# Local attention in an attention-and-FFN kernel: sums of values moved directly behind the next unit's scores

## The chip, the cores and the metric

The kernel runs on one core of a Trainium2 chip. The metric is the device time of one execution in microseconds. TensorE (PE; its weight loads are rows of PEld), VectorE (DVE), ScalarE (ACT), GpSimd (POOL) and SyncE (SP, which issues the transfers) each work through a queue of their own and wait for each other by semaphores.

## The reference, cut to what matters

For 8 batches and 8 heads of 64 columns, 512 local queries see 32 global keys and the local keys at most 32 positions away; 32 global queries see everything. The 8 heads side by side (512 columns) then go through a norm and a feed-forward network of 2048 hidden columns with a residual.

```python
s_g = scale * np.matmul(q_g, k_all.transpose(0, 1, 3, 2))
out_g = np.matmul(sm(s_g), v_all)
mask = np.abs(pos[:, None] - pos[None, :]) <= window      # window = 32
s_ll = np.where(mask, scale * np.matmul(q_l, k_l.transpose(0, 1, 3, 2)), -1e9)
s_lg = scale * np.matmul(q_l, k_g.transpose(0, 1, 3, 2))
out_l = np.matmul(sm(np.concatenate([s_lg, s_ll], axis=-1)), np.concatenate([v_g, v_l], axis=2))
...
xn = (x - mu) / np.sqrt(var + 1e-06) * g_ln
out = x + np.maximum(xn @ w_ch1, 0.0) @ w_ch2
```

## The kernel before

**Units.** Local attention is cut into 64 units (class `Local`): a batch, a pair of heads, one half of 256 local rows. A unit has three stages.

- `scores` (L248): 16 matmuls in the program (32 instructions in the trace) of 64 rows by 32 columns of the array into the left 256 columns of two PSUM banks, `sc[0]` for the pair's first head and `sc[1]` for its second. Then, on VectorE and ScalarE, four reductions with the mask (`p<-sc`, L275) and four exponentials (L285).
- `transposes` (L289): units 8 to 15 on TensorE (`tp`) with a copy by ScalarE, units 16 to 63 as 16 transposes on VectorE (`pt<-p`, L307).
- `values` (L309): 16 matmuls (32 instructions) of 128 rows by 32 columns into a third bank, `pv`; then VectorE writes `x<-pv` (L328, one instruction). At its end `values` loads the operands of the unit after the next (`u<-in_eu`, L245) into the one of two buffers that it has read. After a pair's fourth unit, `finish` stores x (`xs<-x`) and makes the norm: statistics (L189, L191), `rs` by GpSimd and VectorE, and `x<-x` on ScalarE (L202).

The scores' banks, `tp`, `pv` and the chunks' transposes `t` all turn in one PSUM pool of two banks (`ps_a`, tag `att`).

**Chunks.** Rows go through the feed-forward network in nine chunks: 0 to 7 of four tiles of 128 local rows (eight units each), 8 of the global rows. `ffn` loops over 16 slabs f of the hidden columns: `mm1(f)` is 12 matmuls of 512 columns into `ph`, followed by `hh` (ScalarE, L539) and `hl` (VectorE, L540); then come 12 matmuls of `mm2(f-1)` into `acc`. `mm2(f)`, which has `hl(f)` as its weights, thus stands behind `mm2(f-1)` and `mm1(f+1)`. At a chunk's end its output goes out (`out<-ob`, four transfers) and the next chunk's residual comes into the same buffers (`ob<-xs`, four transfers).

**Order.** Units 0 to 7 run ahead of the network. The other units stand in it: while chunk c runs, the units of chunk c+1 are computed, and in chunks 1 to 5 also the first unit of chunk c+2. `PLACES` says where: place 2f is `mm1(f)`, 2f+1 is `mm2(f-1)`; unit n of a chunk starts at int(start + n * period), and its three stages stand 0, 1 and 4 places further (0, 2 and 3 in chunk 0; start 1, period 3.75 in chunks 2 to 6). At place 1 there is no `mm2`, since f is 0 there. The stages are generators of which `ffn` takes a step ahead of each third of `mm1` and each quarter of `mm2`. The order on TensorE and SyncE is the program's; VectorE, ScalarE and GpSimd are ordered by the scheduler.

Of the kernel before, what the change touches and what calls it, by code (L numbers as in the profile page):

```python
# [31 lines left out]

ON_PE = 16

PLACES = {0: (0, 3.5, (0, 2, 3)), 1: (0, 3.4, (0, 1, 4)), 7: (1, 3.5, (0, 1, 2)), 9: (1, 3.75, (0, 1, 4))}
BIG = 3.0e38


# [8 lines left out]
def attention_ffn_kernel(  # L47
# [12 lines left out]
    B, HP, _, _, _ = eu.shape  # L60
# [159 lines left out]
    class Local:  # L220


        def __init__(self, b, hp, half, alone, on_pe):
            self.at = b, hp, half
            self.alone = alone
            self.on_pe = on_pe
            self.next = None

        def bank(self, k, name):

# [18 lines left out]
        def scores(self):  # L249
            half = self.at[2]  # L250
            mn = small.tile([P, 4], F32, name="mn")
            self.sm = small.tile([P, 4], F32, name="sm")
            self.p = self.ap.tile([P, 4, P], F32, name="p", bufs=3)
            sc = [self.bank(h, "sc") for h in range(2)]
            for qb in range(2):
                for g in range(4):
                    gp = slice(g * WIN, (g + 1) * WIN)
                    w = 4 * qb + g
                    k0 = 8 + w + w // 3
                    for h in range(2):  # L260
                        hd = slice(h * D, (h + 1) * D)
                        nc.tensor.matmul(  # L262
                            sc[h][gp, qb * P:(qb + 1) * P],
                            self.e[hd, w * WIN:(w + 1) * WIN],
                            self.e[hd, k0 * WIN:(k0 + 4) * WIN],
                            start=True,
                            stop=True,
                            tile_position=(h * D, g * WIN),
                            skip_group_check=True,
                        )  # L270
            yield
            for h in range(2):
                for qb in range(2):
                    c = 2 * h + qb
                    nc.vector.tensor_tensor_reduce(  # L275
                        out=self.p[:, c],
                        in0=sc[h][:, qb * P:(qb + 1) * P],
                        in1=masks[half, qb],
                        scale=-QSCALE,
                        scalar=BIG,  # L280
                        op0=ALU.add,
                        op1=ALU.min,
                        accum_out=mn[:, c:c + 1],
                    )
                    nc.scalar.activation(  # L285
                        self.p[:, c],
                        self.p[:, c],
                        AF.Exp,
                        bias=mn[:, c:c + 1],  # L289
                        scale=-1.0,  # L290
                        accum_out=self.sm[:, c:c + 1],
                    )
# [15 lines left out]

        def values(self):  # L309
            b, hp, half = self.at  # L310
            pv = self.bank(3, "pv")
            for h in range(2):
                for qb in range(2):
                    for g in range(4):
                        gp = slice(g * WIN, (g + 1) * WIN)
                        nc.tensor.matmul(  # L316
                            pv[gp, qb * P + h * D:qb * P + h * D + D],
                            self.pt[:, 2 * h + qb, gp],
                            self.v[:, 4 * qb + g, h * D:(h + 1) * D],
                            start=True,  # L320
                            stop=True,
                            tile_position=(0, g * WIN),
                            skip_group_check=True,
                        )
            ri = small.tile([P, 4], F32, name="ri")
            nc.gpsimd.tensor_scalar(ri, self.sm, SUM_EPS, None, ALU.add)  # L326
            nc.vector.reciprocal(ri, ri)
            nc.vector.tensor_tensor(  # L328
                self.x[:, :, hp * P:(hp + 1) * P].rearrange("p q (h d) -> p q h d", h=2),
                pv[:, :256].rearrange("p (q h d) -> p q h d", q=2, h=2),  # L330
                ri.rearrange("p (h q) -> p q h", h=2).unsqueeze(3).to_broadcast([P, 2, 2, D]),
                op=ALU.mult,
            )
            if not self.alone and self.next and self.next.next:
                self.next.next.load()
# [141 lines left out]
    def rows_local(b, t):  # L477
        r0 = b * SA + SG + t * P
        return [(slice(0, P), r0, P)]

    def rows_global(bg):
        return [(slice(i * SG, (i + 1) * SG), (bg * BG + i) * SA, SG) for i in range(BG)]

    def transpose_chunk(xn, out, t0=0, nt=None):


        n = len(xn) * P
        nt = nt or len(xn)
        for kt in range(KT):
            t = ps_a.tile([P, 512], F32, name="t", tag="att")  # L490
            for j in range(len(xn)):
                nc.tensor.transpose(  # L492
                    t[:, j * P:(j + 1) * P], xn[j][:, kt * P:(kt + 1) * P], ident
                )
            if t0 == 0:
                u = kt % 2
                if u == 0:
                    his = fpool.tile([P, 2, 512], F32R, name=f"xh{kt}", tag=f"xh{kt}")
                    if nt > 2:
                        los = fpool.tile([P, 2, 512], F32R, name=f"xl{kt}", tag=f"xl{kt}")  # L500
                out.append((his[:, u], los[:, u]) if nt > 2 else (his[:, u, :256], his[:, u, 256:]))
            hi, lo = (a[:, t0 * P:t0 * P + n] for a in out[kt])
            gk = g_sb[:, kt:kt + 1]
            nc.scalar.activation(hi, t[:, :n], AF.Copy, scale=gk)
            nc.vector.scalar_tensor_tensor(
                lo, t[:, :n], gk, f32(hi), ALU.mult, ALU.subtract
            )
            yield
# [87 lines left out]
    def tiles(c):  # L596
        return tiles_of(ready.pop(c))
# [5 lines left out]
    last_chunk = len(chunks) - 1  # L603
# [12 lines left out]
    units = sum(phases, [])  # L616
    need = [sum(u.chunk <= c for u in units) for c in range(len(chunks))]
# [40 lines left out]

    def stages(units):

        for u in units:
            def first(u=u):
                yield from u.scores()

            def second(u=u):
                for _ in u.transposes():
                    pass
                return
                yield

            def third(u=u):
                for _ in values(u):
                    pass
                yield

            yield first, second, third

    queue = list(stages(units[need[0]:]))
    queue.reverse()

# [4 lines left out]
    with tc.manual_schedule(engines={ET.SP}):  # L685
# [6 lines left out]
        with hurry(True):  # L692
            scores = [u.scores() for u in units[:need[0]]]
# [33 lines left out]
    for c, chunk in enumerate(chunks):  # L727
        if c == 0:
            ctx.enter_context(tc.manual_schedule(engines={ET.PE}))
        if chunk is None:  # L730
            rows = [rows_global(bg) for bg in range(NBG)]
        else:
            rows = [rows_local(b, 2 * half + j) for b, half in chunk for j in range(2)]
        want = need[min(c + 1, last_chunk)] + (0 < c < last_chunk - 2)
        count = want - traced["units"]
        traced["units"] = want
        start, period, offs = PLACES.get(c, PLACES[9])
        at = {}
        place = 0
        for n in range(count):  # L740
            for o, run in zip(offs, queue.pop()):
                place = min(max(int(start + n * period) + o, place), 2 * NF - 1)
                at.setdefault(place, []).append(run)

        def stage(f, k, at=at, c=c):
            if c == 0 and k == 0:
                for _ in weights_to(f + SPLIT_AHEAD + 1, LOADS_AHEAD):
                    pass
            for run in at.get(2 * f + k, ()):
                yield from run()  # L750

        nxt = []

        def next_chunk(c=c, nxt=nxt):
            if c + 1 < len(chunks):
                yield from transpose_chunk(tiles(c + 1), nxt)

        ffn(c, xt, rows, stage, next_chunk)
        xt = nxt
# [87 lines left out]
```

## Time and profile before

| | us |
|---|---|
| median of 3 runs | 998.15 |
| lowest and highest | 997.3 and 999.79 |
| the profiled execution | 995.42 |
| its span, first to last instruction | 993.6 |
| TensorE busy in the span | 948.8 |
| VectorE, ScalarE, GpSimd busy | 578.0, 314.7, 44.0 |

Matmuls overlap their own ends, so busy time says little of the pace. What a stretch costs is read from the starts of the instructions behind it.

### The profile page before, as it was taken

To read this page: it belongs to the slowest core of one execution; us is meant where nothing else is said; L and a number is where in the kernel's file an instruction comes from. 1 tells how busy PE (TensorE), PEld (TensorE's weight loads), DVE (VectorE), ACT (ScalarE), POOL (GpSimd) and SP (SyncE) were. 2 spreads that over 40 slices of the span, in tenths; PEclk is the share of its full clock that TensorE was granted. 3 is DMA by queue.
4 is the path that set the end of the run, shared out by engine and by line. 5 is a ranking of instruction groups with operands and counts; after the bars stand their busy time and mean duration, and the time that the engine had idled before them with its cause. 6 is when DMAs were issued, how large, how long until landed. Compare 5 with 4: busy or idle time off the path is not lost.

```text
span 993.6 us, 21066 instructions
## 1 busy us (share of the span) xinstructions
PE 948.8 (95%) x8616; PEld 717.2 (72%) x8616; DVE 578.0 (58%) x1873; ACT 314.7 (32%) x842; POOL 44.0 (4%) x150
## 2 busy tenths in 40 slices
PE   6569999999999999999999999999999989999997
PEld 4347677677777777777777777777777766766796
DVE  4589943666766666766666666766666642222311
ACT  5677743223222223222322222222222231232210
POOL 3000000000000000000000000000000000000000
PEclk9679999999999999999999999999999999999999
DMA  8565632323232224222332224222322344543110
GB/s 357 203 250 203 231 113 85 121 76 119 97 120 75 89 80 149 90 93 71 104 122 84 101 68 146 93 71 93 123 84 86 108 158 150 191 147 136 44 32 22
DMA packets 31872, 118.80 MB, mean 120 GB/s; under 512 B 4256, under 2 KB 6304, under 8 KB 27680
## 3 DMA queue, kind: packets, MB, share of 16 engines
q1 hardware_dynamic: 31776, 117.46, 34.6%
q8 instruction: 68, 1.11, 0.5%
q14 instruction: 28, 0.23, 0.1%
HBM read 99.62 MB, written 17.83 MB: 118 GB/s over the span
## 4 chain that ended last, share of the span: by engine, by line
PE 85%; DMA 3%; DVE 3%; ACT 2%; issue 1%; SPq 0%; POOL 0%; ACTq 0%; DVEq 0%
PE acc L550 37%; PE ph L531 36%; PE sc L262 4%; PE pv L316 3%; DMA raw<-in_wd 2%; PE t L492 1%; PE pv L419 1%; DMA xs<-x 1%; PE sc L371 1%; PE t L407 1%; DVE tmp L142 0%; DVE hl L540 0%; DVE pt L307 0%; DVE tmp L146 0%; ACT p L285 0%
## 5 line engine op out<-in xcount | busy, mean ns | idle before, releaser
L550 PE MATMUL acc<-w,hh 128*128 128x512 f32 x1088 | 342.7, 396 | 0.0
L531 PE MATMUL ph<-xh,w 128*128 128x512 f32 (+1 forms) x1216 | 311.7, 382 | 0.0
L307 DVE STREAM_TRANSPOSE pt<-p 32x128 f32<-32x128 f32 x768 | 232.5, 303 | 62.2 <-ACT p L285 50.1
L531 PEld LDWEIGHTS ph<-xh,w 128*128 128x128 f32 x1216 | 214.0, 188 | 49.8 <-issue 3.1
L550 PEld LDWEIGHTS acc<-w,hh 128*128 128x128 f32 x1088 | 205.7, 189 | 44.4
L550 PE MATMUL acc<-w,hl 128*128 128x512 f32 x544 | 225.7, 415 | 2.9 <-DVE hl L540 2.9
L539 ACT ACTIVATE hh<-ph 128x512 fp32r<-128x512 f32 (+1 forms) x144 | 82.3, 572 | 355.6 <-PE ph L531 354.4
L540 DVE SCALAR_TENSOR_TENSOR hl<-ph,hh 128x512 fp32r<-128x512 f32 (+1 forms) x144 | 94.3, 656 | 164.9 <-ACT hh L539 163.4
L285 ACT ACTIVATE p<-p,mn 128x128 f32<-128x128 f32 x256 | 99.7, 391 | 187.9 <-DVE mn L275 187.9
L531 PE MATMUL ph<-xl,w 128*128 128x512 f32 x512 | 143.4, 401 | 0.0
L550 PEld LDWEIGHTS acc<-w,hl 128*128 128x128 f32 x544 | 102.4, 188 | 32.7 <-issue 7.2
L531 PEld LDWEIGHTS ph<-xl,w 128*128 128x128 f32 x512 | 94.0, 188 | 27.8 <-issue 6.9
L275 DVE CUSTOM_DVE_ANT_0 p<-sc,mask 128x128 f32<-128x128 f32 x256 | 58.9, 285 | 45.4 <-PE sc L262 44.8
L262 PE MATMUL sc<-u 64*32 64x128 f32 x2048 | 58.1, 293 | 13.0 <-DMA u<-in_eu 6.2
L262 PEld LDWEIGHTS sc<-u 64*32 64x32 f32 x2048 | 32.3, 112 | 41.6 <-issue 25.1
L316 PEld LDWEIGHTS pv<-u,pt 128*32 128x32 f32 x2048 | 33.8, 113 | 28.1 <-issue 22.4
L328 DVE TENSOR_TENSOR x<-pv,ri 128x256 f32<-128x256 f32 x64 | 26.8, 420 | 43.6 <-PE pv L316 43.6
L316 PE MATMUL pv<-u,pt 128*32 128x64 f32 x2048 | 45.7, 228 | 3.1 <-ACT pt L301 3.0
L285 ACT ACTIVATION_READ_ACCUMULATOR p<-p,mn 128x1 f32 x256 | 47.9, 187 | 0.0
L326 POOL TENSOR_SCALAR ri<-sm 128x4 f32<-128x4 f32 x64 | 17.4, 272 | 585.1 <-ACT p L285 580.9
L202 ACT ACTIVATE x<-x,rs 128x512 f32<-128x512 f32 x32 | 24.8, 811 | 45.1 <-DMA xs<-x 43.5
L492 PE MATMUL t<-ident,x 128*128 128x128 f32 x136 | 23.1, 290 | 10.1 <-DVE x L207 3.9
(58 smaller groups left out, 442.0 us busy)
## 6 DMA issues: line engine op xcount, KB each, us to landing
u<-in_eu SPq DMA_DIRECT2D x63, 848.0 KB, 4.7
raw<-in_wd SPq DMA_DIRECT2D x16, 1024.0 KB, 5.4
gk<-in_gk SPq DMA_DIRECT2D x8, 1088.0 KB, 5.0
xs<-x SPq DMA_DIRECT2D x32, 256.0 KB, 5.7
ob<-xs SPq DMA_DIRECT2D x32, 256.0 KB, 3.4
out<-ob SPq DMA_DIRECT2D x32, 256.0 KB, 2.1
gv<-in_gv SPq DMA_DIRECT2D x8, 1024.0 KB, 5.0
u<-in_eu SPq DMA_DIRECT2D x1, 512.0 KB, 4.1
```

The source lines that it names most:

```text
L202: nc.scalar.activation(x[:, j, :], x[:, j, :], AF.Identity, bias=rs[:, 1, j:j + 1], scale=rs[:, 0, j:j + 1],)
L262: nc.tensor.matmul(sc[h][gp, qb * P:(qb + 1) * P], self.e[hd, w * WIN:(w + 1) * WIN], self.e[hd, k0 * WIN:(k0 + 4) * WIN], start=True, sto ...
L275: nc.vector.tensor_tensor_reduce(out=self.p[:, c], in0=sc[h][:, qb * P:(qb + 1) * P], in1=masks[half, qb], scale=-QSCALE, scalar=BIG, op0= ...
L285: nc.scalar.activation(self.p[:, c], self.p[:, c], AF.Exp, bias=mn[:, c:c + 1], scale=-1.0, accum_out=self.sm[:, c:c + 1],)
L307: nc.vector.transpose(out=self.pt[rp, :, gp], in_=self.p[gp, :, rp])
L316: nc.tensor.matmul(pv[gp, qb * P + h * D:qb * P + h * D + D], self.pt[:, 2 * h + qb, gp], self.v[:, 4 * qb + g, h * D:(h + 1) * D], start= ...
L328: nc.vector.tensor_tensor(self.x[:, :, hp * P:(hp + 1) * P].rearrange("p q (h d) -> p q h d", h=2), pv[:, :256].rearrange("p (q h d) -> p ...
L492: nc.tensor.transpose(t[:, j * P:(j + 1) * P], xn[j][:, kt * P:(kt + 1) * P], ident)
L531: nc.tensor.matmul(ph[:, :n], w[:, kt, :], xx[kt][:, :n], start=(i == 0), stop=(i == 3 * KT - 1),)
L539: nc.scalar.activation(hh[:, :n], ph[:, :n], AF.Relu)
L540: nc.vector.scalar_tensor_tensor(hl[:, :n], ph[:, :n], 0.0, f32(hh[:, :n]), ALU.max, ALU.subtract)
L550: nc.tensor.matmul(acc[t], a[:, ts], w, start=(f == 0 and i == 0), stop=(f == NF - 1 and i == 2),)
```

## The change

The sums of values of unit n-1 no longer have a stage of their own. They stand directly behind the score matmuls of unit n, and they go into the right half (columns 256 to 511) of that unit's bank `sc[0]` in place of a bank `pv`. The first unit of the queue (unit 8) has no unit ahead; the last local unit (63) and the global units keep their third stage. So 55 units' sums move. Chunk 0 takes nine units in place of eight, and chunk 1 eight in place of nine, with the places of the other chunks. The instructions are as many as before on every engine.

```diff
-PLACES = {0: (0, 3.5, (0, 2, 3)), 1: (0, 3.4, (0, 1, 4)), 7: (1, 3.5, (0, 1, 2)), 9: (1, 3.75, (0, 1, 4))}
+PLACES = {0: (0, 3.5, (0, 2, 3)), 7: (1, 3.5, (0, 1, 2)), 9: (1, 3.75, (0, 1, 4))}
...
-            sc = [self.bank(h, "sc") for h in range(2)]
+            sc = self.sc = [self.bank(h, "sc") for h in range(2)]
...
         def values(self):
             b, hp, half = self.at
-            pv = self.bank(3, "pv")
+
+            pv = self.beside.sc[0][:, 256:] if self.beside else self.bank(3, "pv")
...
-        for u in units:
-            def first(u=u):
-                yield from u.scores()
+
+        for n, u in enumerate(units):
+            before = units[n - 1] if n else None
+            if before and u.chunk == last_chunk and before.chunk < last_chunk:
+                before = None
+            alone = n + 1 == len(units) or u.chunk == last_chunk or units[n + 1].chunk == last_chunk
+
+            def first(u=u, before=before):
+                scores = u.scores()
+                if before and u.chunk < last_chunk:
+                    next(scores)
+                    before.beside = u
+                    for _ in values(before):
+                        pass
+                yield from scores
...
-            yield first, second, third
+            yield (first, second, third) if alone else (first, second)
...
-        want = need[min(c + 1, last_chunk)] + (0 < c < last_chunk - 2)
+        want = need[min(c + 1, last_chunk)] + (c < last_chunk - 2)
```

TensorE, chunk 3, before its second unit's scores. Before, sums and scores stand apart, with three network matmuls between them:

```order
L531 MATMUL ph<-xl_4114,w 128x512 x2
L531 MATMUL ph<-xh_4091,w 128x512 x2
L531 MATMUL ph<-xh_4113,w 128x512 x2
L316 MATMUL pv<-u,pt 32x64 x16
L550 MATMUL acc_4147<-w,hl 128x512
L550 MATMUL acc_4147<-w,hh 128x512 x2
L262 MATMUL sc<-u 32x128 x16
L550 MATMUL acc_4148<-w,hl 128x512
```

The same unit now (line numbers are one higher from L309 on):

```order
L551 MATMUL acc_4101<-w,hl 128x512
L551 MATMUL acc_4101<-w,hh 128x512 x2
L551 MATMUL acc_4102<-w,hl 128x512
L551 MATMUL acc_4102<-w,hh 128x512 x2
L262 MATMUL sc<-u 32x128 x16
L317 MATMUL sc<-u,pt 32x64 x16
L532 MATMUL ph<-xh_4040,w 128x512 x2
L532 MATMUL ph<-xh_4062,w 128x512 x2
```

Scores and sums are one block. At a chunk's head the second unit's scores now stand 24 network matmuls behind the first unit's (one `mm1`, one `mm2`), where before 39 matmuls and a block of sums lay between them; elsewhere 36 or 48 stand between two units.

SyncE's queue at the same chunk's head, before:

```order
L245 DMA u<-in_eu 128x1696
L583 DMA out<-ob 128x512 x4
L559 DMA ob<-xs 128x512 x4
L245 DMA u<-in_eu 128x1696 x3
L342 DMA xs<-x 128x512 x2
```

And now:

```order
L343 DMA xs<-x 128x512 x2
L584 DMA out<-ob 128x512 x4
L560 DMA ob<-xs 128x512 x4
L245 DMA u<-in_eu 128x1696 x4
L343 DMA xs<-x 128x512 x2
```

The load for the chunk's second unit, which stood ahead of the four stores and four loads, stands behind them.

VectorE, third unit of chunk 3, from its last reductions to `hl`, before:

```order
L275 ISA p,mn<-sc,mask_105 128x128
L275 ISA mn 128x1
L307 STREAM_TRANSPOSE pt<-p 32x4x32 x9
L540 SCALAR_TENSOR_TENSOR hl<-ph,hh 128x512
L307 STREAM_TRANSPOSE pt<-p 32x4x32 x7
L327 RECIPROCAL ri<-ri 128x4
L540 SCALAR_TENSOR_TENSOR hl<-ph,hh 128x512
L328 TENSOR_TENSOR x<-pv,ri 128x2x128
```

And now:

```order
L275 ISA p,mn<-sc,mask_105 128x128
L275 ISA mn 128x1
L329 TENSOR_TENSOR x<-sc,ri 128x2x128
L275 ISA p,mn<-sc,mask_96 128x128
L275 ISA mn 128x1
L275 ISA p,mn<-sc,mask_105 128x128
L275 ISA mn 128x1
L307 STREAM_TRANSPOSE pt<-p 32x4x32 x16
L328 RECIPROCAL ri<-ri 128x4
L541 SCALAR_TENSOR_TENSOR hl<-ph,hh 128x512 x2
```

The write of x now stands between the reductions of `sc[1]` and those of `sc[0]`, and both `hl` stand behind all 16 transposes. In a chunk's fourth unit, and in its last one, the norm's statistics stand ahead of the transposes as well.

## Rows read from the trace of the kernel before

**Rows 1.** The page: busy time of TensorE, and its granted clock by slices.

```profile
PE 948.8 (95%) x8616; PEld 717.2 (72%) x8616; DVE 578.0 (58%) x1873; ACT 314.7 (32%) x842; POOL 44.0 (4%) x150
PEclk9679999999999999999999999999999999999999
```

**Rows 2.** Lines L262 and L316: duration of one, ns min/median/max.

```profile
L262 PE MATMUL sc<-u x2048: 266/269/420, 3.8 to 779.5; 64*32 64x128 f32 x187
...
L316 PE MATMUL pv<-u,pt x2048: 219/219/316, 14.3 to 790.9; 128*32 128x64 f32 x187
```

**Rows 3.** TensorE in order of time, chunk 4: start us, us, instruction.

```profile
506.28 1.09 PE L531 MATMUL ph<-xl,w 128*128 128x512 f32 x4
507.22 1.10 PE L531 MATMUL ph<-xh,w 128*128 128x512 f32 x4
508.24 0.65 PE L316 MATMUL pv<-u,pt 128*32 128x64 f32 x32
...
509.16 0.63 PE L550 MATMUL acc<-w,hh 128*128 128x512 f32 x2
509.72 1.06 PE L262 MATMUL sc<-u 64*32 64x128 f32 x32
510.71 0.50 PE L550 MATMUL acc<-w,hl 128*128 128x512 f32 x1
511.05 0.63 PE L550 MATMUL acc<-w,hh 128*128 128x512 f32 x2
...
518.05 0.63 PE L550 MATMUL acc<-w,hh 128*128 128x512 f32 x2
...
520.32 0.67 PE L262 MATMUL sc<-u 64*32 64x128 f32 x32
...
521.96 1.09 PE L531 MATMUL ph<-xh,w 128*128 128x512 f32 x4
```

**Rows 4.** Waits from 173 to 800 us: total us, times, longest.

```profile
PEld sc L262 <- DVE x L328: 4.7, 18, 0.3
```

**Rows 5.** TensorE ahead of the network: scores and sums without network matmuls between.

```profile
25.84 1.17 PE L262 MATMUL sc<-u 64*32 64x128 f32 x32
26.95 0.31 PE L316 MATMUL pv<-u,pt 128*32 128x64 f32 x6
```

**Rows 6.** Head of chunk 3 in order of time: TensorE, SyncE's queue, VectorE.

```profile
393.88 0.67 PE L262 MATMUL sc<-u 64*32 64x128 f32 x32
...
400.18 1.10 PE L531 MATMUL ph<-xh,w 128*128 128x512 f32 x4
...
394.60 1.75 SPq L559 DMA_DIRECT2D ob<-xs  x4
...
397.23 5.10 DVE L307 STREAM_TRANSPOSE pt<-p 32x128 f32<-32x128 f32 x16 [1.09 <-ACT p L285]
```

**Rows 7.** Landing of the load of u issued at 403.8, nothing ahead of it.

```profile
DMA to landing us min/median/max: 4.9/4.9/4.9
```

**Rows 8.** Four loads of ob, and the load of u behind them: issue, landing.

```profile
L559 SPq DMA_DIRECT2D ob<-xs x4: 326/428/430, 131.3 to 132.6; - x4
...
L245 SPq DMA_DIRECT2D u<-in_eu x1: 333/333/333, 134.0 to 134.0; - x1
...
DMA to landing us min/median/max: 6.4/6.4/6.4
```

**Rows 9.** Chunk 0: TensorE in order; waits 58 to 170; window: PE busy, PEclk, DMA.

```profile
120.68 0.62 PE L550 MATMUL acc<-w,hh 128*128 128x512 f32 x2
...
126.45 0.39 PE L550 MATMUL acc<-w,hl 128*128 128x512 f32 x1
...
PEld sc L262 <- DVE x L328: 2.4, 3, 1.5
...
123.00:125.00 2.00, 2.00 (x33) 0.50 0.79 221
```

**Rows 10.** VectorE, statistics of a norm in chunk 4.

```profile
532.58 1.29 DVE L189 BATCH_NORM_STATS2 st<-x 128x6 f32<-128x512 f32 x2
```

More of the change, by code (lines that the diff above doesn't have):

```diff
@@ L226, in __init__ @@
             self.on_pe = on_pe
-            self.next = None
+            self.next = self.beside = None
         def bank(self, k, name):
```

## The prediction

> **What bounds the kernel now.** I read the page first: TensorE is busy for 95% of the span, and its granted clock is full (2.4 GHz) in nearly every slice [rows 1]. So what counts is the order of starts on TensorE. Next I read that order in a steady chunk [rows 3]. Four network matmuls take 0.94 us from start to start (506.28 to 507.22), so one takes 0.234. A block of small matmuls breaks this pace twice, going in and coming out, and where an unbroken pace would have put a later matmul tells what the block costs. Last I looked at what TensorE waits for [rows 4], and at the head of a chunk [rows 6], where the change puts two units closest together. The sum is made against the profiled execution, 995.42 us, of which 993.6 is span; that is 2.7 below the median of the runs, 998.15, and I carry the difference over.
>
> **One block in place of two.** The second `hh` matmul behind the sums should start at 507.22 + 0.94 + 0.23 = 508.39 without them; it starts at 509.16 [rows 3]. So the sums cost 0.77 us. From 518.05, where two `hh` matmuls, sums, four matmuls, scores and four matmuls follow, ten matmuls alone would lead to 520.39, and the trace has 521.96: both blocks cost 1.57, and so scores 0.80. Taken apart: scores start 0.09 us later than a network matmul would (509.72 against 509.16 + 0.47 = 509.63). The burst takes 0.67 - 0.27 = 0.40 from first to last start [rows 2, 3]. From a burst's last start to the next network matmul is 0.20 (509.72 + 1.06 - 0.27 = 510.51 to 510.71), and the second network matmul follows 0.34 behind the first (511.05), 0.10 too late. The sums show the same entry: 508.24 against 507.22 + 0.94 = 508.16.
>
> With sums directly behind scores three things go: 0.20 (leaving the scores), 0.10 (the late second matmul) and 0.09 (entering the sums). What comes is the step from scores to sums. Ahead of the network it is there: the last of 32 scores starts at 25.84 + 1.17 - 0.27 = 26.74, the sums at 26.95, so 0.20 [rows 5]. The saving is 0.39 - 0.20 = 0.19 us a unit, and for 55 units **10.5 us**. The ends: nothing if the step costs as much as what goes, 21 if it costs nothing; the row shows the very step, so I take it.
>
> **Waits for a bank that go.** Scores wait in the middle of their burst where `x<-pv` has not yet left a bank of the shared pool: 18 times from 173 to 800 us [rows 4]. At 509.72 the burst lasts 1.06 in place of 0.67; the matmul at 511.05 would stand at 509.16 + 0.47 + 0.47 = 510.10 less 0.24, at 509.86, so these scores cost 1.19, and the wait 0.39. The sums take no bank now, and a unit's two banks were read one unit earlier. So 18 * 0.39 = **7.0 us** go.
>
> In chunk 0 three such waits stand [rows 9]. From 120.68 two and then six network matmuls would lead to 122.55, and the trace has 126.45: 3.9 lost, less 0.8 for the scores themselves, 3.1. Of it the wait has 1.5; most of the rest, 1.6, is the clock: it was granted at 0.50, its lower level of 1.2 GHz, from 123 to 125 us, right behind that wait. The other two waits have 0.9 of the 2.4 us. That makes 4.0; against it, chunk 0's second score bank now waits for the copy of `tp` by a busy ScalarE, as the sums do now, and the exponentials come a little later for the transposes. I take **3.5**, between 0 and 7.
>
> **The head of a chunk, a new wait.** In chunks 1 to 6 the first unit's scores and the second's are now only 24 network matmuls apart. Before, the matmul at 400.18 stood behind these 24, 6.30 us from the scores at 393.88 [rows 6]. The sums lengthen the block by 0.20 for the step in, 0.65 - 0.22 = 0.43 for the burst [rows 2, 3] and 0.15 for the way out (508.67 to 509.16 less 0.34), in place of the 0.20 out of the scores: 0.58. With the entry, the second unit's scores would start at 393.88 + 6.30 + 0.58 + 0.09 = 400.85 and the sums behind them 0.60 later, at 401.45. Two things are late for that.
>
> - The sums need the first unit's transposes, which end at 397.23 + 5.10 = 402.33 [rows 6]. The write of x now stands among the reductions, but ScalarE is the slower of the two on a unit's four pairs of reduction and exponential, so I leave the transposes where they are. This alone is a wait of 0.9.
> - The scores need `u`, whose load is now issued when the sums at the head are done, and behind the four loads of `ob`, whose issue ends at 394.60 + 1.75 = 396.35. Alone such a load lands after 4.9 [rows 7]: at 401.3, 0.4 late. Issued behind four loads of `ob` it took 6.4 [rows 8]: at 402.8, 1.9 late; the sums then wait no more.
>
> The Trainium skill ("DMA: Bandwidth & Descriptors", Queues, rings and completion order) says that SyncE's transfers share one row of rings and that each DMA engine takes descriptors in ring order. By it `ob` drains first and the wait is the longer one, some 2.0 with the semaphore; without it the 0.9 of the transposes would stand. Over six heads that is 12 against 5.4, and the gain below would be 4.2 or 10.8. The slow load of rows 8 agrees with it.
>
> The case of rows 8 is the nearer one, but there `u` was issued 0.9 us after the last `ob` and the other traffic differed, so I take 1.6 a head: 6 * 1.6 = **9.6 us lost**, ends 5.4 and 12.
>
> **Smaller losses.** The fourth unit of a chunk has the norm's statistics (1.29 us, [rows 10]) ahead of its transposes, and both `hl` behind them. By my estimate, from the scores' start s: reductions from s + 0.76, x at 1.31 to 1.73, two reductions to 2.2, statistics to 3.6, transposes (5.10) and a second aggregation to 8.9, `hl` at 9.7. TensorE wants it as a weight at s + 9.46 (1.18 for the block, 0.34 for the first step, 34 more matmuls). So 0.25 is lost in each of six chunks, **1.5**, ends 0 and 4. Units without statistics have 0.5 to spare. At the end of chunk 0, unit 16 stands where nothing stood; `rs` of unit 15's norm comes behind its transposes, at s + 9.9, and the rows of x are normed 1.6 later, while TensorE wants them at 9.9: **1.7**, ends 0 and 3. Elsewhere 48 matmuls lie there and the norm is in time. And of six new waits of up to 2 us I let one drop the clock, at the price of chunk 0: **1.6**.
>
> **Sum.** 10.5 + 7.0 + 3.5 - 9.6 - 1.5 - 1.7 - 1.6 = 6.6 us less: 988.8 for a profiled execution like this one, 991.5 for the median.
>
> **Rivals.**
>
> *No new wait at the heads.* `u` lands early enough and the transposes come forward, as the load of 4.9 us half suggests; the clock stays up too. Then 10.5 + 7.0 + 3.5 - 1.5 - 1.7 = 17.8: 977.6, or 980.4 by the median. Against it: the transposes' 5.10 us are in every unit of these chunks and nothing in the change shortens them.
>
> *The sums wait for VectorE, and most is given back.* `hl` behind 16 transposes has 0.5 to spare in units two and three of a chunk; if the write of x pushes the exponentials by 0.7 us, 0.2 is lost 12 times and 0.7 more 6 times at the fourth units, 6.6 in all, and nothing is left of the gain: 995.4, or 998.1 by the median. For it: VectorE's order puts `hl` last. Against: ScalarE's four exponentials take longer than the reductions and the write of x together.
>
> *Slower: the heads cost more than everything saves.* Each head waits 2.0 for `u`, and the clock falls each time, with 1.6 to pay as at 121 us: 3.6 * 6 = 21.6 against 21.0 - 3.2 = 17.8 saved, 3.8 more: 999.2, or 1002 by the median. It decides from 3.0 a head for no gain, and from 3.5 for slower. For it: a wait of 1.5 us stood ahead of the low clock in chunk 0 [rows 9]. Against: the granted clock is full in the rest of the chunks.
>
> *The change does not save what it says.* The step from scores to sums costs 0.39 in the network, where a block starts behind 512-column matmuls and the sums go into the bank that the scores have just written. Then 10.5 go from the sum: 3.9 slower, 1002.1 by the median. Against it: the step of rows 5.
>
> **How the numbers follow.** A measurement of this kernel can tell about 0.3%, 3 us, from no change. Forecast (gain of 3 to 11): 0.55. No wait at the heads: 0.18. Given back on VectorE: 0.14. Heads and clock: 0.09. No saving in the block: 0.04. So faster 0.73, same 0.14, slower 0.13. The predicted time is that of the forecast, 991.5. The range leaves out half of the best case below (980) and most of the slower cases above (999).
>
> **What would show it.** Right: in the steady chunks scores and sums start 0.60 apart and cost 1.38 together (0.77 + 0.80 - 0.19); no wait of scores for `x`; a wait of 0.9 to 2 us of scores for `u`, or of sums for `pt`, once at the head of each of chunks 1 to 6. Wrong: a block of 1.57; waits for `pt` or `hl` in every unit; a granted clock under 1.0 in the middle slices; no wait at the heads.

## The result, and the profile after

| | before | after |
|---|---|---|
| median of 6 runs each, us | 998.67 | 987.40 |
| lowest and highest | 995.30, 1000.31 | 986.18, 991.45 |
| the profiled execution | 995.42 | 991.45 |
| its span | 993.6 | 989.6 |

The ratio is 0.9896, with a 95% interval of 0.987 to 0.9922: 1.0% faster. The profiled execution of after is the slowest of its six, 4 us above their median. Before's profiled execution is 3 us below its median. So the two traces differ by 4.0 us, where the medians differ by 11.3: the traces show where time went, but not all of what the median gained. Line numbers are one higher from L309 on.

The page of after: busy time of the engines, and TensorE's granted clock by slices, as in [rows 1].

```profile
PE 938.9 (95%) x8616; PEld 724.4 (73%) x8616; DVE 573.7 (58%) x1873; ACT 316.9 (32%) x842; POOL 44.3 (4%) x150
PEclk9679999999989999999999999999999999999999
```

TensorE in order of time, chunk 4 (start us, us, instruction), as in [rows 3]:

```profile
515.64 0.40 PE L551 MATMUL acc<-w,hl 128*128 128x512 f32 x1
515.88 0.63 PE L551 MATMUL acc<-w,hh 128*128 128x512 f32 x2
516.44 0.67 PE L262 MATMUL sc<-u 64*32 64x128 f32 x32
517.03 0.65 PE L317 MATMUL sc<-u,pt 128*32 128x64 f32 x32
517.62 1.20 PE L532 MATMUL ph<-xh,w 128*128 128x512 f32 x4
518.66 1.09 PE L532 MATMUL ph<-xl,w 128*128 128x512 f32 x4
```

Scores and sums start 0.59 apart, and the block costs 518.66 - 515.88 - 6 * 0.234 = 1.38, where the two blocks cost 1.57 [rows 3].

Waits from 173 to 800 us (total us, times, longest), as in [rows 4]:

```profile
PEld sc L262 <- issue: 28.9, 47, 3.7
PE sc L262 <- DMA u<-in_eu: 11.5, 6, 3.3
```

The first row is of weight loads that wait for nothing that the profile shows. No row of scores waiting for x is left; the 18 waits of [rows 4] are gone. In their place scores wait six times for `u`, once in each of chunks 1 to 6. The worst of the six, at the head of chunk 3, beside [rows 6]: TensorE, SyncE's queue, VectorE, and the landing of the load of u issued at 391.90.

```profile
388.14 0.67 PE L262 MATMUL sc<-u 64*32 64x128 f32 x32
...
394.56 0.63 PE L551 MATMUL acc<-w,hh 128*128 128x512 f32 x2
398.50 1.23 PE L262 MATMUL sc<-u 64*32 64x128 f32 x32 [3.31 <-DMA u<-in_eu]
...
390.10 1.75 SPq L560 DMA_DIRECT2D ob<-xs  x4
391.90 9.24 SPq L245 DMA_DIRECT2D u<-in_eu  x2
...
391.50 5.11 DVE L307 STREAM_TRANSPOSE pt<-p 32x128 f32<-32x128 f32 x16 [0.76 <-ACT p L285]
...
DMA to landing us min/median/max: 6.5/6.5/6.5
```

The load of u lands at 391.90 + 6.47 = 398.37 (the row rounds to 6.5) and the scores start at 398.50. The transposes had ended at 396.61. Where these scores run slowly (1.23 us in place of 0.67) the granted clock was down. Windows of about a chunk each (PE, PEld, DVE, ACT and POOL busy; then the granted clock, the busy share of the DMA engines and GB/s):

```profile
283.00:388.00 105.00, 102.56 (x843) 80.22 (x841) 66.98 (x232) 27.04 (x83) 3.67 (x12) 0.97 0.28 93
388.00:493.00 105.00, 101.69 (x903) 79.65 (x903) 68.30 (x242) 28.73 (x88) 3.67 (x12) 0.98 0.28 90
493.00:599.00 106.00, 104.86 (x923) 82.11 (x922) 69.25 (x243) 28.65 (x88) 3.67 (x12) 1.00 0.31 104
```

Behind three of the six waits (2.5, 3.4 and 2.1 us) the clock fell to its lower level for a while; behind the other three (1.4, 1.2 and 1.4) it stayed full.

A ledger of the traces follows: from the start of one chunk's last transposes `t` to that of the next, in us. The last column is the kernel of the first experiment below.

| | before | after | place 1.25 |
|---|---|---|---|
| start to the end of chunk 0 | 172.27 | 169.47 | 167.44 |
| chunk 1 | 110.32 | 103.95 | 102.54 |
| chunk 2 | 105.15 | 107.88 | 102.47 |
| chunk 3 | 105.17 | 107.41 | 102.46 |
| chunk 4 | 105.17 | 103.80 | 102.47 |
| chunk 5 | 105.16 | 103.99 | 102.47 |
| chunk 6 | 102.58 | 105.57 | 101.87 |
| from there to the end | 187.8 | 187.5 | 188.5 |

Chunks 2, 3 and 6, where the clock fell, are longer than before; chunks 4 and 5 are shorter; chunk 1, which has one unit less, is shorter by 6.4.

One sentence ahead of the prediction has to be corrected. SyncE's order is the program's only ahead of the network. In the network it is the scheduler's, and that is why the loads of `ob`, which the program writes at f = 14, stand at the chunk's head.

### The profile page after: what moved, and what is told of

It is laid out like the page before. It is cut to its first block, busy times and chain, and to the rows that moved or that the text cites. A ratio compares the mean times of both kernels' runs of the same rounds, so it can differ in the third digit from the quotient of the medians.

```text
span 989.6 us, 21066 instructions
## 1 busy us (share of the span) xinstructions
PE 938.9 (95%) x8616; PEld 724.4 (73%) x8616; DVE 573.7 (58%) x1873; ACT 316.9 (32%) x842; POOL 44.3 (4%) x150
## 4 chain that ended last, share of the span: by engine, by line
PE 75%; DMA 8%; DVE 6%; SPq 2%; ACT 1%; issue 1%; POOL 0%; DVEq 0%; ACTq 0%
PE acc L551 33%; PE ph L532 32%; DMA u<-in_eu 4%; PE sc L262 3%; PE sc L317 3%; DMA raw<-in_wd 2%; DMA out<-ob 2%; SPq L560 1%; PE t L493 1%; PE pv L420 1%; DVE tmp L142 1%; DVE tmp L146 1%; PE sc L372 1%; PE t L408 1%; DVE w L152 1%
## 5 line engine op out<-in xcount | busy, mean ns | idle before, releaser
L532 PEld LDWEIGHTS ph<-xh,w 128*128 128x128 f32 x1216 | 216.3, 190 | 49.6 <-issue 2.3
L551 PE MATMUL acc<-w,hl 128*128 128x512 f32 x544 | 221.8, 408 | 0.5 <-DVE hl L541 0.5
L532 PEld LDWEIGHTS ph<-xl,w 128*128 128x128 f32 x512 | 97.1, 190 | 25.5 <-issue 1.8
L275 DVE CUSTOM_DVE_ANT_0 p<-sc,mask 128x128 f32<-128x128 f32 x256 | 63.0, 284 | 52.6 <-PE sc L262 46.9
L262 PE MATMUL sc<-u 64*32 64x128 f32 x2048 | 51.7, 297 | 22.5 <-DMA u<-in_eu 18.7
L262 PEld LDWEIGHTS sc<-u 64*32 64x32 f32 x2048 | 31.1, 113 | 46.0 <-issue 37.0
L317 PE MATMUL sc<-u,pt 128*32 128x64 f32 x1760 | 37.2, 227 | 0.0
L317 PEld LDWEIGHTS sc<-u,pt 128*32 128x32 f32 x1760 | 28.1, 113 | 11.4 <-issue 11.2
L493 PEld LDWEIGHTS t<-ident,x 128*128 128x128 f32 x136 | 16.9, 147 | 19.0 <-issue 6.7
```

What stands on the lines that cost most here:

```text
L262: nc.tensor.matmul(sc[h][gp, qb * P:(qb + 1) * P], self.e[hd, w * WIN:(w + 1) * WIN], self.e[hd, k0 * WIN:(k0 + 4) * WIN], start=True, sto ...
L275: nc.vector.tensor_tensor_reduce(out=self.p[:, c], in0=sc[h][:, qb * P:(qb + 1) * P], in1=masks[half, qb], scale=-QSCALE, scalar=BIG, op0= ...
L317: nc.tensor.matmul(pv[gp, qb * P + h * D:qb * P + h * D + D], self.pt[:, 2 * h + qb, gp], self.v[:, 4 * qb + g, h * D:(h + 1) * D], start= ...
L493: nc.tensor.transpose(t[:, j * P:(j + 1) * P], xn[j][:, kt * P:(kt + 1) * P], ident)
L532: nc.tensor.matmul(ph[:, :n], w[:, kt, :], xx[kt][:, :n], start=(i == 0), stop=(i == 3 * KT - 1),)
L551: nc.tensor.matmul(acc[t], a[:, ts], w, start=(f == 0 and i == 0), stop=(f == NF - 1 and i == 2),)
```

## The experiments

No kernel leaves anything of the reference out. Ratios are to the kernel before, measured beside it on the same chip; the chips differ between some of the experiments, so kernels are best compared by their ratios.

**The second unit one place later.** In place of 24 network matmuls, 36 stand between the first and the second unit's scores. By the rounding of places the sixth unit moves one place too; after has no wait of TensorE there.

```diff
-PLACES = {..., 9: (1, 3.75, (0, 1, 4))}
+PLACES = {..., 9: (1.25, 3.75, (0, 1, 4))}
```

> The changed kernel with the second unit of a chunk at place 5 in place of 4 (start 1.25 in place of 1), so that 36 network matmuls lie between the first two units' scores and not 24. Theory (at the heads of chunks 1 to 6 TensorE waits about 2 us each for u, which comes too late for 24 matmuls, and some of these waits drop the clock): the scores at a head start 2.8 us later, so the waits for u fall from some 12 us in all to under 2, the granted clock stays at 1.00 in the middle slices, and the time falls by 10 to 16 us from the changed kernel's 987.4, to 971 to 977. Rival (the heads cost nothing that matters, since the chunk's end waits for something else): within 3 us of 987.

Measured: 973.17 us (972.06 to 973.91), ratio 0.9767 (0.974 to 0.9794). The wait for `u` is in no row of chunks 1 to 6, the clock is full there, and chunks 2 to 5 last 102.47 each. The prediction's terms give 105.17 - 8 * 0.19 - 3 * 0.39 = 102.5 for such a chunk with nothing lost at its head. So all that after loses in the steady chunks lies at their heads: 18.3 us in the two traces (chunks 1 to 6 of the ledger). By the ratios the two kernels differ by 12.9 as a whole; that is the whole kernel, with a chunk 0 that ends 2.0 earlier in this trace and an end that lasts 1.0 longer.

**SyncE in the program's order**, so that the loads of `ob` no longer stand ahead of the load of `u`.

```diff
-            ctx.enter_context(tc.manual_schedule(engines={ET.PE}))
+            ctx.enter_context(tc.manual_schedule(engines={ET.PE, ET.SP}))
```

> The changed kernel with SyncE's queue in the order of the program from chunk 0 on: the four loads of ob then stand at the end of their chunk, no longer at its head in front of the load of u. Theory (u is late because it stands behind the loads of ob): u lands about 4.9 us after its issue, in time for the second unit's scores; what is left at a head is a wait of the sums for the transposes, 0.9 us, and the time falls by 5 to 12 us, to 975 to 982. Rival (the transposes or the load itself, and not what stands ahead of it, set the heads): waits of 2 us stay at the heads and the time stays within 3 us of 987.

Measured: 976.24 us (974.33 to 977.32), ratio 0.9793 (0.9767 to 0.9818). The head of chunk 3 in this kernel (TensorE, then SyncE's queue), and its waits from 173 to 800 us:

```profile
386.22 0.67 PE L262 MATMUL sc<-u 64*32 64x128 f32 x32
386.82 0.31 PE L317 MATMUL sc<-u,pt 128*32 128x64 f32 x6
387.76 0.63 PE L317 MATMUL sc<-u,pt 128*32 128x64 f32 x26 [0.63 <-DVE pt L307]
...
375.16 2.44 SPq L584 DMA_DIRECT2D out<-ob  x4
380.56 8.20 SPq L245 DMA_DIRECT2D u<-in_eu  x2
...
PEld sc L317 <- DVE pt L307: 4.8, 6, 0.9
```

In the program's order the loads of `ob` were issued some 17 us ahead of the head (360.19 to 362.75, with the first unit's scores at 379.25). With no `ob` ahead of it, u is in time and the scores wait no more. What is left is the smaller of the two waits in the prediction: the sums wait for the transposes, six times. Such a block costs 2.29 in place of 1.37, so 0.92 each; the prediction had 0.9 for "the transposes alone".

**The loads of ob cut in halves.**

```diff
-                    nc.sync.dma_start(ob[ps, t, :], xs[r0:r0 + nr, :])
+                    for hs in (slice(0, DM // 2), slice(DM // 2, DM)):
+                        nc.sync.dma_start(ob[ps, t, hs], xs[r0:r0 + nr, hs])
```

> The kernel after, with each of the four loads of ob cut in two halves of 256 columns: the same bytes, eight issues of 0.43 us where four stood ahead of the load of u, so that this is issued some 1.7 us later; nothing is left out. It asks whether the granted clock falls where the wait at a head is long. Theory 1 (the wait grows by 1 to 1.7, to 2.2 to 5 us, and the clock falls at all six heads where it fell at three of six, at some 2.2 us each): 6 * 1.4 + 3 * 2.2 = 15 more, 1002 (997 to 1006). Theory 2 (the wait grows, but the clock falls by chance, at about half of the heads): 8 more, 995 to 996. Rival (the load of u lands when the bytes ahead have drained, not by when it was issued): no longer wait, 986 to 989.

Measured: 980.91 us (978.59 to 983.39), ratio 0.9834 (0.9806 to 0.9861), 6 us faster than after by the ratios, which none of the three expected. The edit did not do what its expectation says. SyncE's queue at the head of chunk 3:

```profile
381.59 1.98 SPq L561 DMA_DIRECT2D ob<-xs  x4
383.62 0.43 SPq L245 DMA_DIRECT2D u<-in_eu  x1
384.09 2.66 SPq L561 DMA_DIRECT2D ob<-xs  x4
```

The scheduler put the load of u behind four of the eight halves, so half the bytes of `ob` stand ahead of it. By accident this is a middle case between after and the program's order. Mean of the six heads of chunks 1 to 6, in us; the scores' own place is 6.97 behind the first unit's scores:

| ahead of the load of u | issued after the first scores | issue to landing | wait, six heads in all |
|---|---|---|---|
| all of `ob` (after) | 2.71 | 6.11 | 12.0 |
| half of it (this kernel) | 2.17 | 5.81 | 6.9 |
| nothing (SyncE in the program's order) | 1.31 | 4.46 | 0 |

So u is late on two counts of about the same size, both from the loads of `ob` in its queue: it is issued 1.4 us later, since SyncE issues in order, the four loads of `ob` take 1.75 us to issue and wait for the stores from the same buffer to land (nine times from 170 to 800 us, 12.8 in all); and it takes 1.65 longer to land. The Trainium skill ("DMA: Bandwidth & Descriptors", Queues, rings and completion order) says that SyncE's transfers share one row of rings, taken in ring order. The trace agrees in part: the landing is longer with `ob` ahead (5.2 to 7.0, against 4.2 to 4.7 with nothing), but with half the bytes ahead and the other half issued right behind it spreads as widely, 4.9 to 5.5 at four heads and 6.8 and 6.9 at two. So it does not follow the bytes ahead alone, and what parts the two groups is not shown.

The waits became shorter, so the two theories on the clock were not tested as planned. In this kernel it fell behind a wait of 1.9 us and stayed full behind one of 2.4. Over the traces of after, of this kernel and of the next one there are 18 heads. The clock fell at 5 of the 6 with a wait over 1.9, and at none of the 12 with a wait of 1.8 or less. That is a count and no rule, and other rows of the study break it. In the kernel before, TensorE waits 2.2 us for `hl` in chunk 1 and the clock stays full (first row). And at the start of the chunk of global rows all twelve traces have the same two waits of TensorE, 1.15 us for `gp` on VectorE and 1.5 us for `gp` on ScalarE. The clock stayed full behind them in four: before (the second and third rows, a window that is mostly idle and the one behind it), after, the next kernel, and the kernel before with chunk 1's places from 1. It fell to 0.5 in the other eight; the last row is that of the second unit one place later, whose stretch to the end is 188.5 in the ledger against 187.5 of after.

```profile
173.00:283.00 110.00, 107.81 (x980) 81.05 (x978) 75.47 (x269) 30.06 (x96) 3.89 (x13) 1.00 0.30 101
...
815.00:817.00 2.00, 0.55 (x15) 1.00 1.03 348
817.00:819.00 2.00, 1.86 (x12) 1.00 0.96 337
...
704.00:800.00 96.00, 93.33 (x823) 72.38 (x822) 53.86 (x181) 25.51 (x69) 3.22 (x10) 0.98 0.32 107
```

So the length of a wait alone does not decide. What does is not shown.

**Scores and sums apart again**, with a third of `mm1` or a quarter of `mm2` between them; all else as after.

```diff
                     next(scores)
                     before.beside = u
+                    yield
                     for _ in values(before):
```

> The changed kernel with the sums one step of the network (three or four matmuls) behind the scores, still in the free half of their bank. The neighbourhood alone is undone, for all units but the first of a chunk, 48 of 55. Theory (the block saves 0.19 us a unit by one entry and one exit fewer): 48 * 0.19 = 9 us more than the changed kernel, 993 to 1000, with scores at 0.80 and sums at 0.77 again, and no wait of scores for x. Rival (what the change gains comes from the bank that the sums no longer take): the time stays within 3 us of the changed kernel's 987.

Measured: 1001.82 us (996.5 to 1005.56, 12 runs), ratio 1.0046 (1.0024 to 1.0068). That is 14 more than after (15 by the ratios), more than expected. The profiled run, 996.7, is one of the fastest, so what the slower ones lost is not in a trace; the waits at the heads are in this kernel too, with one fall of the clock in its trace. Hence the same step without the heads' wait:

**Apart, with the place of 1.25.**

> The heads without their wait (second unit of a chunk 36 network matmuls behind the first, 973.2 us when it was alone) and, on top, a step of network matmuls between scores and sums of 48 units; nothing is left out of the computation. It prices the one block apart from everything at the heads. Theory (a block costs 1.37, sums and scores apart 0.80 + 0.78 = 1.58, and nothing else hangs on it): 48 * 0.205 = 9.8 us more, 983.0 (981 to 986). Rival 1 (the 14 us that the same step cost in the kernel after are the price of the block, not of its heads): 987. Rival 2 (the block saves nothing): 973.

Measured: 987.7 us (986.02 to 991.39), ratio 0.9905 (0.988 to 0.9931). By the time the first rival is right; the trace divides it. TensorE in chunk 3 of this kernel:

```profile
420.50 0.63 PE L551 MATMUL acc<-w,hh 128*128 128x512 f32 x2
421.06 0.67 PE L262 MATMUL sc<-u 64*32 64x128 f32 x32
421.66 1.20 PE L532 MATMUL ph<-xh,w 128*128 128x512 f32 x4
422.79 0.65 PE L317 MATMUL sc<-u,pt 128*32 128x64 f32 x32
423.37 1.20 PE L532 MATMUL ph<-xl,w 128*128 128x512 f32 x4
```

Scores cost 0.80 and sums 0.77 here. From the end of chunk 0 to the end of chunk 6 this kernel takes 622.93 us and the one with a single block 614.28. The 8.65 more stands over the 41 units that are apart there (49 in all; the expectation says 48). A wait of 0.6 for `u` in chunk 1 is in it; the rest is 0.20 a unit, as the theory has it. In chunks 2 to 5, without a wait, it is 1.36 for seven units, 0.19 each. Most of the rest is in chunk 0, which ends 5.84 us later: 1.1 at its last transposes, 1.6 from eight units apart, and 3.1 in waits and clock. The granted clock fell to 0.5 for 3.4 us from 117.1 on, behind a wait of 1.9 for ScalarE, and in chunk 0 of the kernel with the place alone it did not; that is about 1.7 of the 3.1. So the block saves 0.2 a unit, and chunk 0 changed by several us in these experiments.

**The sums directly behind the scores, but in a bank of their own.**

```diff
-            pv = self.beside.sc[0][:, 256:] if self.beside else self.bank(3, "pv")
+            pv = self.bank(3, "pv")
```

> The changed kernel with the sums directly behind the scores, but in a bank of their own from the shared pool of two. Theory (the free half is what lets the sums follow at once): the sums now need the bank of the scores just made, which is read 1.2 us after the scores' start, where the sums would start at 0.6; a wait of 0.6 to 0.8 in each of 55 blocks, 30 to 45 us more than the changed kernel, 1015 to 1035. Rival (banks come free in time): within 5 us of the changed kernel.

Measured: 1053.15 us, one run. A unit in chunk 3 (TensorE in order), and the waits from 173 to 800 us:

```profile
443.40 0.67 PE L262 MATMUL sc<-u 64*32 64x128 f32 x32
444.82 0.65 PE L317 MATMUL pv<-u,pt 128*32 128x64 f32 x32 [0.75 <-DVE mn L275]
...
PE pv L317 <- DVE mn L275: 45.9, 44, 1.4
```

The pool turns in two banks, and both hold the scores just written. So the sums wait for reductions of one of them in 44 units of this window, with 0.75 to 1.39 us of idle time in the two kinds that were read (here 0.75), where 0.20 is the step without a wait. The direction was right and the size too small: 61 us more span than after, of which these 44 waits are 46 and a longer chunk 0 is 16. The free half of the scores' bank is thus not a detail of the change; without it the block is not to be had with two banks.

**Eight units in chunk 0 and nine in chunk 1, as before**, with the place of 1.25 elsewhere.

```diff
-PLACES = {0: (0, 3.5, (0, 2, 3)), 7: ...
+PLACES = {0: (0, 3.5, (0, 2, 3)), 1: (0.6, 3.4, (0, 1, 4)), 7: ...
...
-        want = need[min(c + 1, last_chunk)] + (c < last_chunk - 2)
+        want = need[min(c + 1, last_chunk)] + (0 < c < last_chunk - 2)
...
+            alone = alone or n == 7
+            before = None if n == 8 else before
```

> The heads without their wait, and chunk 0 takes eight units as in the kernel before, chunk 1 nine (period 3.4, start 0.6); unit 15 keeps a third stage with a bank of its own, so 54 units' sums stand behind scores; nothing is left out. It prices the ninth unit in chunk 0. Theory (at the end of chunk 0 the norm of unit 15 is late by 1.05 us because of unit 16's transposes, and the nine units' places cost chunk 1 nothing): the first transposes of chunk 0's end last 0.33 in place of 1.38, less 0.2 for one block more that is cut in two: 972.3 (970.5 to 974). Rival 1 (the ninth unit also crowds ScalarE in chunk 0, where some 4 us of waits stand): 969. Rival 2 (nine units crowd chunk 1, with three spacings of 36 matmuls more): 975 to 977.

Measured: 976.9 us (976.34 to 978.36), ratio 0.9795 (0.9771 to 0.982), 3.7 above the first experiment; by the ratios 2.8, with intervals that overlap. The time is the second rival's; the traces show why. At the end of chunk 0 the first four transposes last 0.33, as expected. Chunk 1 takes 105.72 in place of 102.54. The chunk has the scores of one unit more, which stand alone and cost 0.80; the rest, 2.4, is one wait in chunk 1 that after does not have and before has too. The page's waits from 173 to 283 us, here and in the kernel before:

```profile
PE acc L551 <- DVE hl L541: 2.2, 1, 2.2
...
PE acc L550 <- DVE hl L540: 2.2, 1, 2.2
```

With places that start at 0, chunk 1's first unit has its scores ahead of the first `mm1`. Its 16 transposes then stand ahead of the first `hl`, and the first `mm2` is only 24 matmuls away. Two runs test whether it is the place or the number of units.

**The kernel before, with chunk 1's places from 1.**

```diff
-PLACES = {0: (0, 3.5, (0, 2, 3)), 1: (0, 3.4, (0, 1, 4)), ...
+PLACES = {0: (0, 3.5, (0, 2, 3)), 1: (1, 3.3, (0, 1, 4)), ...
```

> The kernel before with one part of the change alone, its places in chunk 1: the nine units start at place 1 (period 3.3) in place of 0 (period 3.4), so that the first unit's scores stand behind the chunk's first 12 network matmuls and not ahead of them. Nothing is left out. In the trace of before, the first mm2 of chunk 1 waits 2.2 us for hl, which VectorE computes behind the 16 transposes of that first unit (184.26 us, matmul at 184.97, 2.59 behind the one ahead). Theory (that wait is the place's doing, and the change took it away beside all else): chunk 1, from last transposes to last transposes, 110.3 - 2.4 = 107.9 us, and the whole 2.4 less than before (0.9976; hardly to be told by the time alone). Rival (the wait moves to another hl or to a bank): chunk 1 still 109.5 to 111.

Measured: 993.57 us (990.61 to 997.03, 10 runs), ratio 0.9966 (0.9947 to 0.9985). No wait for `hl` is left in chunk 1, which takes 107.45. This part of the change alone is worth 2.9 us in the trace and 3.4 by the times.

**Eight and nine units, with chunk 1's places from 1.**

```diff
-1: (0.6, 3.4, (0, 1, 4))
+1: (1, 3.3, (0, 1, 4))
```

> The kernel with eight units in chunk 0 and nine in chunk 1 (976.9 us) with one difference: the first unit of chunk 1 starts at place 1 in place of 0, all other places the same. Nothing is left out. Theory (the 2.6 us that the first mm2 of chunk 1 waits for hl there come from place 0, not from the number of nine units): that wait is gone, chunk 1 lasts 105.7 - 2.4 = 103.3 to 103.9 us, the whole 974.5 (973 to 976). Rival (nine units crowd VectorE in chunk 1): the wait appears at another hl, 976 to 978.

Measured: 975.41 us (975.21 to 975.73), ratio 0.9791 (0.9772 to 0.9811), inside the theory's range, though chunk 1 is not. TensorE in order, chunk 1's second unit:

```profile
173.03 0.67 PE L262 MATMUL sc<-u 64*32 64x128 f32 x32
...
179.43 0.67 PE L262 MATMUL sc<-u 64*32 64x128 f32 x32
180.02 0.52 PE L317 MATMUL sc<-u,pt 128*32 128x64 f32 x6
181.54 0.63 PE L317 MATMUL sc<-u,pt 128*32 128x64 f32 x26 [0.99 <-DVE pt L307]
```

The wait for `hl` (2.4 us lost) is gone, and chunk 1 shortens by 1.0, to 104.74: places 1 and 4 put 24 matmuls between the first two units, and the wait for the transposes, known from the heads, takes 1.5 (the block costs 2.87 in place of 1.37).

**Both remedies of the heads.**

> Both remedies of the heads at once: the place 1.25, and SyncE in the program's order in the network (loads of ob near the chunk's end); nothing is left out. Theory 1 (the two remedies take away the same wait, and the place alone took all of it): as the place alone, 973.2 (971.7 to 974.7). Theory 2 (SyncE's order also serves chunk 0, whose first to last transposes were 1.9 us shorter with it; it was slower than the place only by six waits of 0.9 for the transposes at the heads): 971.3 (969.5 to 972.5).

Measured: 971.27 us (970.17 to 975.59), ratio 0.9742 (0.9716 to 0.9767). It is the fastest kernel of the study, 2.6% below the one before. Its chunk 0 ends 1.0 earlier than with the place alone. But the intervals of the two overlap, so that the second theory is not shown. The place alone already leaves no wait at the heads of chunks 1 to 6.

## Why the prediction was right

The time, 987.4 against 991.5, lies in the range, and the direction and the mechanism hold: a saving in every unit, taken back in part at the heads. How near the number came is partly luck. Terms were wrong by up to 4.5 us in both directions. And the sum is one of profiled executions, 6.6 forecast and 4.0 measured, while the medians gained 11.3 (10.4 by the ratio): what the other runs of after lost less is in no trace. The sizes, term by term, for the profiled execution (plus is time saved):

| term | forecast | measured | from |
|---|---|---|---|
| one block in place of two | +10.5 | +11.2 | (1.576 - 1.373) * 55 |
| waits for a bank, 173 to 800 us | +7.0 | +6.8 | what the late scores of before cost over 0.80 |
| chunk 0, its waits | +3.5 | +3.0 | what is left of 2.8, see below |
| first `hl` of chunk 1 | none | +2.4 | 2.59 - 0.23 |
| heads, wait for `u` | -9.6 | -12.0 | six heads |
| heads, clock | -1.6 | -6.1 | chunks 2, 3 and 6 |
| `hl` behind the statistics | -1.5 | 0 | no wait for `hl` |
| norm at the end of chunk 0 | -1.7 | -1.05 | 1.38 against 0.33 |
| sum | +6.6 | +4.3 | the two spans: +4.0 |

*The block.* The step from scores to sums, read ahead of the network [rows 5], is 0.20 in the network too (517.03 against a last score start of 516.44 + 0.40). The experiment with sums apart at the place of 1.25 gives 0.20 a unit. The Trainium skill ("TensorEngine Tiling (Array Packing)", Key Properties) says that changing the tiling mode drains TensorE. The trace is in keeping with that: the instructions are as many as before, and the merged order has one change less between 64-row tiles, 128-row by 32-column tiles and the full array. That the 0.20 is a drain is not shown; no run puts small matmuls of one mode against another.

*The bank.* All waits for `x` are gone, and the bank of its own shows what would have stood in their place.

*Chunk 0.* It gained 2.8 us. With 1.6 for eight blocks, 0.8 for the ninth unit's scores and 1.05 for the norm, 3.0 is left for its waits. The fall of the clock at 123 us, 1.6 of the forecast's 4.0, is not in the trace of after. New waits stand there (transposes on TensorE wait 1.4 us for ScalarE's exponentials at 101.2), so the sum is right and its parts were not all foreseen. Against after, other kernels of the study ended this chunk 3.9 us earlier to 3.8 later, and 15.9 later with a bank of its own.

*The heads.* The step was right: u behind four loads of `ob` took 6.1 us on the mean (5.2 to 7.0), where [rows 8] gave 6.4, and 4.5 with nothing ahead. The mean wait is 2.0, at the upper end that was given. The 1.6 was a compromise between two rows, of which the one behind `ob` was the right one. The transposes end 8.47 behind the first scores, and 8.45 was taken.

*The clock.* Mis-sized: it fell three times in the profiled execution, not once, at 1.6 to 2.9 us each. The chunks with a fall lose more than the wait: chunk 2 is 107.88 - 102.46 - 2.5 = 2.9 longer, chunks 3 and 6 1.6 each. That run is the slowest of six, and by the ratios the kernel without the heads' wait is 12.9 faster (forecast: 11.2). That the others had fewer falls is not shown: their granted clocks over the whole run are 0.975 to 0.983 against 0.976, and the run with 0.975 took only 987.77 us. The reason that the forecast gave, a fall behind one of six waits because one stood behind the wait at 121 us, gives no count of falls, since the length of a wait alone does not decide. The slower rival, heads and clock each time for 21.6 us, was thus nearer in this trace than its chance of 0.09 said: 18.1.

*The write of x and `hl`.* No wait came. For a fourth unit with scores at 425.23 the `hl` ends at 434.62, 9.39 behind them, and the matmul that reads it starts at 434.92, 9.69 behind:

```profile
427.31 1.28 DVE L189 BATCH_NORM_STATS2 st<-x 128x6 f32<-128x512 f32 x2
428.51 0.17 DVE L191 BATCH_NORM_AGGREGATE mv<-st 128x2 f32<-128x6 f32 x1
428.59 2.48 DVE L307 STREAM_TRANSPOSE pt<-p 32x128 f32<-32x128 f32 x8
...
433.96 0.66 DVE L541 SCALAR_TENSOR_TENSOR hl<-ph,hh 128x512 fp32r<-128x512 f32 x1
...
434.92 0.40 PE L551 MATMUL acc<-w,hl 128*128 128x512 f32 x1
```

The estimate had 9.7 and 9.46. One matmul too few was counted, 0.23, and VectorE starts each operation a little before the last one's shown end. Both are small, and so was the term.

*The norm at the end of chunk 0.* The wait is there, in the third and fourth of the first transposes, 1.05 in place of 1.7.

*The step that was left out.* The change also moves chunk 1's places from 0 to 1. The trace of before shows the 2.2 us wait of the first `mm2` of chunk 1 for `hl` (at 184.97), and the diff shows the line; the prediction read the line only for the number of units. It is worth 2.4 to 3.4 us. It offset half of the error in the other direction at the heads' clock.

*The rivals.* No wait at the heads: not in after, but one number makes it so, and then the time is 973, lower than the 980 worked out. Of these 7 us, 3.9 are the two terms that were not there (`hl` behind the statistics, 1.5) or not seen (the first `hl` of chunk 1, 2.4); chunk 0 ends 2.0 earlier than in after; the rest was not traced. Given back on VectorE: no wait for `hl`. The block saves nothing: fell with the step of 0.20.

## What to carry to other kernels

When work is moved together, list what the first of it releases (here the buffer and load of u, and the transposes) and count the distance to the next use at the tightest place, not at the usual one; twelve matmuls more of distance there were worth some 13 us by the ratios, about as much again as the 10 that the change itself brought. Read each changed line of a table for every place that it moves: here one line removed a wait that had nothing to do with the idea. A fall of the clock is not to be priced from the length of a wait alone: behind the same two waits it came in eight traces of twelve. Two adjacent blocks of small matmuls among large ones save one way out and one way in, and cost one step between them; both are to be read as starts, never as busy time.

## What the runs showed of the hardware

A load of 128x1696 landed 4.46 us after its issue with nothing ahead of it (mean of six), 6.11 behind four loads of 128x512 on the same queue, and with half of those bytes ahead and half behind after 4.9 to 5.5 four times and 6.8 and 6.9 the other two times.

Among 128x512 matmuls at 0.234 us each, a burst of 64-row tiles directly followed by one of 128-row by 32-column tiles cost 1.37 us, and the two apart 1.57.

TensorE's granted clock does not follow the length of a wait alone. At 18 heads of three traces it fell behind 5 of 6 waits over 1.9 us, and the chunks of after with a fall lost 1.6 to 2.9 us beyond the wait; behind none of 12 shorter ones. But it stayed full behind a wait of 2.2 us in chunk 1 of the kernel before, and behind the same two waits of 1.15 and 1.5 us it fell in eight of twelve traces and stayed full in four.
